# Seven block products for the second channel layer, its factors folded into weights and biases, in a sinkhorn-attention and ResMLP kernel

## The chip, the cores and the metric

The kernel runs on one core of one Trainium2 chip. The metric is the device time of one execution in microseconds (us). All runs were interleaved with runs of the kernel before, so each ratio compares runs of the same rounds. A run is called fast or slow by its time against the fastest of the same kernel; the slow ones here (three of e5_wtok, three of e18_wtok_nopool) showed a lower mean granted TensorE clock than the fast one beside them.

In the text PE is the matrix engine and PEld its weight load, DVE the vector engine, ACT the scalar engine, POOL the general engine. Work has to pass between them all the time: in this kernel PE's results go to accumulator banks (names in `_ps`, and `ch_a` to `ch_c` in the changed kernel), and ACT or DVE empties (evacuates) each bank before PE uses it again.

## The reference, cut to what matters

```python
# attention: x[b] (768 x 512), from 8 heads; 4 batches
a1  = alpha1 * x + beta1
tok = einsum('ts,bsd->btd', w_tok, a1)         # 768 x 768 token mixing
u   = x + lam * tok
a2  = alpha2 * u + beta2
ch  = maximum(a2 @ w_ch1, 0) @ w_ch2           # 512 -> 2048 -> 512
out = u + lam * ch
```

`lam`, the `alpha`s and the `beta`s are vectors of 512 channels.

## The kernel before

It works on batch 0's attention, then, for b = 1 to 3, on the attention of batch b laid between the matrix work of batch b-1 (hidden layer `h_ps`, second layer `ch_ps`), and at the end on batch 3's layers alone. The token mixing and both layers touched by the change, cut:

```python
def moe_tok(b, kts, done=False):               # kts: row tiles of 128 tokens
    for n in range(len(kts) + 1):
        if n < len(kts):
            if not done: tok_part(b, kts[n])   # 6 matmuls of 512 columns on x
            tps = tok_of[(b, kts[n])]
            dve.tensor_tensor(tps, tps, a1lB[:], ALU.mult)         # alpha1*lam
        if n > 0:
            kt = kts[n - 1]
            dve.tensor_tensor(u32[kt][:], tok_of[(b, kt)], u32[kt][:], ALU.add)
            act.copy(u16_of[b][:, kt, :], u32[kt][:])
# u32 holds x + beta1*lam*(row sums of w_tok) beforehand, computed by POOL
def moe_h(b, hf, which=range(HT)):             # hf: half of the rows, 384
    ...
        for ci in range(CT):                   # 4 matmuls of 384 columns
            pe.matmul(hps[:], W1p[:, ci, m*128:(m+1)*128], a2T_of[b][hf][:, ci, :], ...)
        act.activation(hT_of[(b, hf)][m], hps[:], AF.Relu)
def moe_ch(b, hf, kks=range(3)):
    ...
        for m in range(HT):                    # 16 matmuls of 512 columns
            pe.matmul(cps[:], hT[m][:, kk*128:(kk+1)*128], W2p[:, m, lo:hi], ...)
        dve.tensor_tensor(cps[:], cps[:], lamB[:, lo:hi], ALU.mult)
        dve.tensor_tensor(ost[:, lo:hi], cps[:], u_of[b][kt][:, lo:hi], ALU.add)
        ...                                    # two output DMAs
# batch 0 / batch 1, in PE's order:
    for kk in range(2):
        moe_ch(0, 0, (kk,))                    # second layer of batch 0 laid between
        mix_k(1, gs=((0, 1), (2,))[kk])        # batch 1's keys
        for h4 in range(2 * kk, 2 * kk + 2):
            turn_q(1, h4, dve.tensor_copy)     # and queries
```

The softmax here doesn't subtract the row's maximum and nothing guards it: scores larger than these inputs give would overflow.

## Time and profile before

| view | before |
|---|---|
| time, median (range) | 269.02 us (268.74 to 269.11) |
| busy share of PE / DVE / ACT / POOL | 96 / 58 / 47 / 35% |
| first real product of the opening (`pj_ps`) | 11.34 us |
| first `h_ps` | 42.5 us |
| first `v_ps` of batch 2 | 105.7 us |
| end of the last matmul, span | 262.5 us, 266.8 us |

The page's first part (busy time of each engine, share of the span, instructions), kernel before:

```profile
span 266.8 us, 5147 instructions
PE 257.3 (96%) x2049; PEld 141.6 (53%) x2059; DVE 154.8 (58%) x333; ACT 125.8 (47%) x232; POOL 92.6 (35%) x100
```

The chain of waits that ended last, as shares of the span by engine. It is almost all PE:

```profile
PE 89%; ACT 4%; DVE 4%; issue 1%; DMA 1%; DVEq 0%; ACTq 0%
```

Two stretches, from the first `h_ps` to batch 2's first `v_ps`, and from there to the last matmul. The columns are the stretch, its length, then each engine's busy time in it (number of instructions), and last the granted clock, the DMA share and GB/s:

```profile
42.50:105.70 63.20, 62.94 (x490) 34.68 (x493) 44.31 (x88) 30.45 (x58) 27.91 (x28) 1.00 1.04 154
105.70:262.50 156.80, 156.06 (x1059) 82.90 (x1062) 77.28 (x150) 71.12 (x134) 36.67 (x33) 1.00 0.50 81
```

PE idles 0.26 us in the first stretch and 0.74 us in the second, and `--waits` lists no wait of PE over its threshold of 0.15 us in either; DVE and ACT have a third to a half of the time free. Groups of instructions that the change touches (busy us, mean ns of one | idle time before them, and what ended it):

```profile
L65 ACT ACTIVATE hTa<-h_ps 128x384 bf16<-128x384 f32 x96 | 45.9, 492 | 67.7 <-PE h_ps L65 66.6
L65 DVE TENSOR_TENSOR ch_ps<-ch_ps,lamB 128x512 f32<-128x512 f32 (+2 forms) x25 | 16.9, 676 | 62.8 <-PE ch_ps L65 60.1 <-issue 2.6
L65 DVE TENSOR_TENSOR tok_ps<-tok_ps,a1lB 128x512 f32<-128x512 f32 x24 | 16.6, 693 | 7.7 <-PE tok_ps L65 7.6
L65 POOL TENSOR_SCALAR u<-b1lB,rs 128x512 f32<-128x512 f32 x18 | 28.9, 1612 | 64.7 <-DVE ost L65 60.1 <-ACT et L65 3.9 <-DVE red L65 0.6
```

The timeline of the opening (start, length, engine, operation, and in brackets the idle time just before and what ended it): the normalised matrix P is done by DVE, and PE, which has been idle, starts.

```profile
11.08 0.21 DVE L65 TENSOR_TENSOR P<-P,csum 32x64 f16<-32x64 f32 x1
11.34 0.34 PE L65 MATMUL pj_ps<-ident,P 32*8 32x8 f16 x8 [1.25 <-DVE P L65]
```

### The profile page before, as it was taken

Reading aid. Unit: us, or ns where it says so; the run is one execution under the profiler, and the core shown is the slowest. Engines: PE = TensorE matmul, PEld = TensorE weight load, DVE = VectorE, ACT = ScalarE, POOL = GpSimd, SP = SyncE. Lnnn points to the kernel's source line nnn. Section 1 sums busy time; section 2 is a strip of 40 time slices with the busy share of each in tenths; the row PEclk is TensorE's granted clock in tenths of the full one; section 3 lists DMA queues with packets and bytes.
Section 4 is the critical chain, followed back from the end, with each engine's and each line's share of the span. In section 5 each row is a group of like instructions: output and inputs, shape, how many; then the busy total and the mean of one; then the engine's idle time right before and its main releaser. Section 6 shows DMA issues by size and latency. Waiting matters only on the chain.

```text
span 266.8 us, 5147 instructions
## 1 busy us (share of the span) xinstructions
PE 257.3 (96%) x2049; PEld 141.6 (53%) x2059; DVE 154.8 (58%) x333; ACT 125.8 (47%) x232; POOL 92.6 (35%) x100
## 2 busy tenths in 40 slices
PE   7799999999999999999999999999999999999993
PEld 3467745565565444554565444554565445545542
DVE  6878687639567966722585867704675962042033
ACT  3376767642585312980375404970474305505600
POOL 8524789103585615008918125002409000000000
PEclk9999999999999999999999999999999999999999
DMA  6999999989999544499996342492200422012012
GB/s 80 183 208 252 206 211 207 209 209 118 206 165 146 115 83 120 115 83 95 207 196 135 61 100 80 118 109 51 81 1 2 86 71 79 2 39 79 2 39 79
DMA packets 62423, 30.88 MB, mean 116 GB/s; under 512 B 48888, under 2 KB 58112, under 8 KB 62400
## 3 DMA queue, kind: packets, MB, share of 16 engines
q0 software_dynamic: 23024, 15.60, 39.1%
q1 hardware_dynamic: 39376, 14.96, 32.7%
q8 instruction: 16, 0.26, 0.4%
q14 instruction: 7, 0.06, 0.1%
HBM read 32.78 MB, written 8.65 MB: 155 GB/s over the span
## 4 chain that ended last, share of the span: by engine, by line
PE 89%; ACT 4%; DVE 4%; issue 1%; DMA 1%; DVEq 0%; ACTq 0%
PE ch_ps L65 31%; PE h_ps L65 30%; PE tok_ps L65 12%; PE x_ps L65 5%; PE sc_ps L65 4%; ACT kT L65 2%; PE v_ps L65 2%; PE k_ps L65 1%; PE q_ps L65 1%; ACT et L65 1%; DVE csum L65 1%; DVE P L65 1%; PE m_ps L65 1%; DVE rsum L65 1%; PE wtok_ps L65 1%
## 5 line engine op out<-in xcount | busy, mean ns | idle before, releaser
L65 PE MATMUL h_ps<-a2T,W1p 128*128 128x384 bf16 x512 | 93.4, 326 | 0.2
L65 ACT ACTIVATE hTa<-h_ps 128x384 bf16<-128x384 f32 x96 | 45.9, 492 | 67.7 <-PE h_ps L65 66.6
L65 PE MATMUL ch_ps<-W2p,hTa 128*128 128x512 bf16 (+2 forms) x290 | 65.9, 370 | 0.5
L65 PEld LDWEIGHTS <-W1p 128*128 128x128 bf16 x512 | 47.5, 98 | 30.3 <-issue 0.9
L65 DVE TENSOR_TENSOR ch_ps<-ch_ps,lamB 128x512 f32<-128x512 f32 (+2 forms) x25 | 16.9, 676 | 62.8 <-PE ch_ps L65 60.1
L65 POOL TENSOR_SCALAR u<-b1lB,rs 128x512 f32<-128x512 f32 x18 | 28.9, 1612 | 64.7 <-DVE ost L65 60.1
L65 PEld LDWEIGHTS <-hTa 128*128 128x128 bf16 x300 | 28.7, 98 | 32.4
L65 PE MATMUL tok_ps<-x,w_tokT 128*128 128x512 f16 x144 | 32.1, 379 | 0.0
L65 POOL TENSOR_TENSOR u<-x,u 128x512 f32<-128x512 f16 x22 | 25.4, 1190 | 18.2 <-DVE x L65 17.3
L65 ACT ACTIVATE et<-sc_ps 96x768 f16<-96x768 f32 x32 | 24.9, 807 | 11.7 <-PE sc_ps L65 11.7
L65 ACT CAST u<-u 128x512 f16<-128x512 f32 x24 | 14.8, 618 | 25.7 <-DVE u L65 25.7
L65 PE MATMUL ch_ps<-W2p,hTb 128*128 128x512 bf16 (+2 forms) x100 | 25.0, 371 | 0.0
L65 PEld LDWEIGHTS <-w_tokT 128*128 128x128 f16 x180 | 14.8, 97 | 16.1
L65 DVE TENSOR_TENSOR tok_ps<-tok_ps,a1lB 128x512 f32<-128x512 f32 x24 | 16.6, 693 | 7.7 <-PE tok_ps L65 7.6
L65 DVE CAST kT<-k_ps 64x512 f16<-64x512 f32 x24 | 16.5, 688 | 3.4 <-PE k_ps L65 3.0
L65 DVE TENSOR_TENSOR x<-x_ps,recip 96x512 f16<-96x512 f32 (+2 forms) x32 | 17.6, 554 | 0.9
L65 DVE TENSOR_TENSOR u<-tok_ps,u 128x512 f32<-128x512 f32 x24 | 16.4, 689 | 1.7
L65 ACT ACTIVATE hTb<-h_ps 128x384 bf16<-128x384 f32 x32 | 15.3, 497 | 3.8 <-PE h_ps L65 3.4
L65 DVE TENSOR_TENSOR ost<-ch_ps,u 128x512 f32<-128x512 f32 (+2 forms) x25 | 16.6, 665 | 0.6
L65 POOL DMA_DIRECT2D qn<-in_q_dram x18 | 15.4, 872 | 4.2 <-PE q_ps L65 3.4
L65 PEld LDWEIGHTS <-hTb 128*128 128x128 bf16 x100 | 9.6, 98 | 10.9
L65 PEld LDWEIGHTS <-et 96*128 96x128 f16 (+2 forms) x288 | 12.4, 99 | 4.6 <-issue 1.2
(95 smaller groups left out, 214.0 us busy)
## 6 DMA issues: line engine op xcount, KB each, us to landing
out_dram<-ost SPq DMA_DIRECT2D x23, 192.0 KB, 2.2
raw<-in_v_dram POOLq DMA_DIRECT2D x8, 384.0 KB, 8.2
raw<-in_k_dram POOLq DMA_DIRECT2D x8, 384.0 KB, 10.7
vscr<-vA SPq DMA_DIRECT2D x6, 384.0 KB, 4.4
Vs<-vscr SPq DMA_DIRECT2D x6, 384.0 KB, 7.5
W1p<-in_moe_w_ch_dram POOLq DMA_DIRECT2D x4, 512.0 KB, 10.5
W2p<-in_moe_w_ch_dram POOLq DMA_DIRECT2D x4, 512.0 KB, 18.6
qn<-in_q_dram POOLq DMA_DIRECT2D x12, 128.0 KB, 5.8
```

What stands on the lines that cost most here:

```text
L65: ins = getattr(self.eng, name)(*args, **kwargs)
```

## The change

The intent is less work on PE, which is the bound. Take two row tiles of the hidden activations (2 x 2 blocks A11 to A22) and the 2 x 2 blocks B11 to B22 of W2: Strassen's scheme in Winograd's form needs seven block products in place of eight, at the price of four sums S1 to S4 per row pair and four combinations T1 to T4 of W2 once. For this lam is multiplied into W2 (scaled by 1024 to keep fp16 accurate), alpha2 into W1, and W1 times beta2 becomes a bias of the ReLU; `a1 = alpha1*lam*x + beta1*lam` is formed once per batch in fp16 (`xa`), so that one operation per tile finishes u. POOL has almost no tensor work left. Batch 0's attention is taken head pair by head pair. w_tok is no longer sorted by DVE but turned with 128-column loads and then 32-column loads over the tail. The core of the diff:

```diff
-                pe.transpose(pst[:, tt*128:(tt+1)*128], wtp[ks // 2][:, tt, ks % 2, :], ident16[:])
+            for rows, at in ((slice(0, 128), 96 * ks), (slice(96, 128), TAIL + 32 * ks)):
+                for tt in range(NT):
+                    pe.transpose(pst[rows, tt*128:(tt+1)*128],
+                                 wt16[:, tt, at:at + rows.stop - rows.start], ident16[:])
...
-    spin(psb([128, 512], FT, "spin_ps")[:], 7)     # fillers
+    spin(psb([128, 512], FT, "spin_ps")[:], 12)
...
+    def affine(b, lo, hi, eng, kts=slice(0, NT)):
+        eng.tensor_tensor(xa, x, a1l16..., ALU.mult)
+        eng.tensor_tensor(xa, xa, b1l16..., ALU.add)
...
+            for mm in range(2):                    # h_ps now 256 columns per m
+                act.activation(hT[:, m, :], hps[:, mm, :], AF.Relu, bias=hbias[:, m:m + 1])
...
+    def moe_sums(b, th):                           # 4 x 1024 elements on DVE
+        dve.tensor_tensor(S1, A21, A22, ALU.add)
+        dve.tensor_tensor(S2, S1, A11, ALU.subtract)
+        dve.tensor_tensor(A21, A11, A21, ALU.subtract)
+        dve.tensor_tensor(S4, A12, S2, ALU.subtract)
...
+        product(pa, A11, B11, True, False); take(u11, pa)   # 8 matmuls of 256 columns
+        product(pb, A12, B21, True, True);  take(u11, pb)   # take: u += ps/1024 on DVE
+        product(pa, S2, T2, False, False);  take(u12, pa)
+        product(pc, S1, T1, True, False);   take(u22, pc)
+        product(pa, S3, T3, False, False);  take(u22, pa)
+        product(pc, S4, B22, False, True);  take(u12, pc)
+        product(pa, A22, T4, False, True);  take(u21, pa)
...
-    for kk in range(2):
-        moe_ch(0, 0, (kk,))
-        mix_k(1, gs=((0, 1), (2,))[kk])
-        ... turn_q(1, h4, dve.tensor_copy)
+    for n in range(3):
+        mix_k(1, gs=(n,), share=(2, 0, 2))
+        turn_q(1, n, act.copy)
+        moe_h(0, 1, range(2 + n, 3 + n))
+    ...
+    for n in range(4): scale_w2(n)                 # W2 is ready only after this
+    combine_w2()
```

## The prediction

> **What bounds it now.** The page's busy table has PE at 96% of the span, DVE 58%, ACT 47%. The chain of waits is 89% PE: ch_ps 31%, h_ps 30%, tok_ps 12%. In that chain 64 h_ps matmuls of 384 columns take 10.40 us (162.5 ns each) and 36 tok_ps of 512 columns take 7.77 us (216 ns): 2.4 columns per ns plus about 2.5 ns per matmul. That agrees with the Trainium skill, "TensorE: Matmul & The Clock Gate" (section on 56 against 53.3 ns). Sixteen x_ps matmuls of 65 columns take 0.51 us, loads included, so loads hide behind 256 columns, which should cost about 109 ns. PE idles 1.3 us before pj_ps at 11.34 us, about 1 us in batch 0, about 2 us per batch 1 to 3 (at ACT kT), and 4 us of tail.
>
> **PE, removed and added.**
> - Second layer: 8 block products become 7; about 82.9 us of ch_ps becomes 672 x 109 = 73.4 us: -9.5.
> - h_ps: 512 x 162.5 becomes 768 x 109: +0.7.
> - w_tok: 36 more transposes of 128 moving columns: +2.0.
> - hbias: 64 one-column matmuls at 27.5 ns (as rs_ps: 36 in 0.99 us) +1.8, rs_ps -1.0.
> - Fewer filler matmuls and one q turn moved into the opening: -1.0.
> Net -7.0 us.
>
> **What takes it back.**
> 1. Opening: two 1x512 fp32 products (0.75 us each, as u<-b1lB,rs,x) enter the normalisation chain on DVE. pj_ps moves from 11.3 to about 12.7 us: +1.4.
> 2. DVE. Added: 48 sums of 128x1024, 4 W2 scalings and 4 combinations of 2048, the affine of x. The Trainium skill, "VectorE: DVE Perf Modes" (perf-mode tier table), gives tensor_tensor on 16-bit SBUF operands two elements per cycle; this trace has no such operation, but its 768-element fp16 copy from PSUM (545 ns) runs at that rate. Estimates: 0.69 us per sum (33 us), 1.2 us per W2 operation (10 us), affine 15 us, W1 scaling 3 us. 84 evacuations of 256 columns at 0.43 us (36 us) replace 33 us. Removed: one tok_ps pass (-16 us), a2T scaling and sorting (-12 us). DVE goes from 155 to about 186 us.
> 3. From the start of the first h_ps to the end of batch 1's tok and last ch, DVE has about 57 us of work against 57 us on PE, in bursts: the W2 block (10 us) precedes the first x_ps evacuations, and tok waits for the affine. I expect 4 to 6 us of new PE idle. In batches 2 and 3, reuse of bank ch_a waits for a DVE evacuation within 0.87 us.
> ACT (about 140 us) and POOL (under 30 us) stay off the chain.
>
> **Sum.** 269.0 - 7.0 + 1.4 + about 5 (batch 0/1) + about 1 - 3 (idle of batches 2 and 3 partly removed) = about 266. Range 260.5 to 270.5. Chances: faster by over 2% 0.33, within 2% 0.60, slower 0.07.
>
> **What would show it.** ch_ps groups total about 73 us at 109 ns spacing; pj_ps near 12.7 us; first h_ps near 45.5 us (42.6 before); batches 2 and 3 take about 57 us (58.7); last batch's h and ch about 40 us (41.5); DVE near 186 us, sums near 0.69 us; waits of PE loads on DVE (u, x, xa) grow.
>
> **What would make it wrong.** Sums or W2 operations at one element per cycle: slower. DVE bursts hidden better than I think: about 260. Loads not hidden at 256 columns: 275 or more.

## The result, and the profile after

The changed kernel took 276.92 us (median of four fast runs, 276.13 to 277.49) against 269.05 us for the kernel before in the same rounds: ratio 1.029, 95% interval 1.026 to 1.032. A ratio here is the mean time of one kernel's fast runs over that of the other's of the same rounds, so it is not quite the ratio of the medians. The prediction had 266.0 us, 0.989 of before; the result is 6 us above the top of its range. The profiled executions have spans of 266.8 and 275.7 us, 8.9 us apart.

The page's first part, kernel after:

```profile
span 275.7 us, 6448 instructions
PE 260.1 (94%) x2693; PEld 201.5 (73%) x2693; DVE 177.7 (64%) x384; ACT 146.4 (53%) x303; POOL 37.3 (14%) x54
```

The chain of waits: PE has lost 19 points of the span, and DVE and ACT have gained 18, although they are busy for only 64 and 53% of it.

```profile
PE 70%; DVE 14%; ACT 12%; issue 2%; POOL 0%; ACTq 0%; POOLq 0%; DVEq 0%
```

The same two stretches:

```profile
47.20:114.50 67.30, 61.42 (x621) 47.34 (x621) 52.12 (x100) 38.44 (x80) 8.47 (x11) 1.00 0.88 120
114.50:271.60 157.10, 153.56 (x1471) 123.35 (x1468) 93.36 (x193) 84.96 (x184) 7.84 (x11) 1.00 0.59 82
```

PE idles 5.88 us in the first (0.26 before) and 3.54 us in the second (0.74). The groups that answer to those of before:

```profile
L66 ACT ACTIVATE hT<-h_ps,hbias 128x256 f16<-128x256 f32 x192 | 77.7, 489 | 25.1 <-PE h_ps L66 23.5
L66 DVE SCALAR_TENSOR_TENSOR u<-ch_a,u 128x256 f32<-128x256 f32 x48 | 20.1, 420 | 8.4 <-PE ch_a L66 8.3
L66 DVE TENSOR_TENSOR S<-S,hT 128x1024 f16<-128x1024 f16 x12 | 8.2, 681 | 0.1
L66 DVE TENSOR_TENSOR xa<-x,a1l 128x768 f16<-128x768 f16 (+1 forms) x9 | 7.3, 816 | 0.0
L66 DVE TENSOR_TENSOR W2p<-W2p,lam 128x2048 f16<-128x2048 f16 x4 | 4.6, 1221 | 0.0
```

The opening. P is ready 1.3 us later than before, as predicted; but twelve filler matmuls already stand in PE's queue in front of `pj_ps`, which starts 1.5 us after P is done.

```profile
11.39 2.76 PE L66 MATMUL spin_ps<-ident 128*128 128x512 f16 x12
12.40 0.21 DVE L66 TENSOR_TENSOR P<-P,csum 32x64 f16<-32x64 f32 x1
14.08 0.34 PE L66 MATMUL pj_ps<-ident,P 32*8 32x8 f16 x8
```

PE's waits in the whole run, the longest in total first, cut (us in all, times, longest):

```profile
PE ch_a L66 <- DVE u L66: 2.7, 6, 0.7
...
PE h_ps L66 <- ACT hT L66: 1.1, 1, 1.1
PE ch_a L66 <- DVE S L66: 1.1, 1, 1.1
```

And a piece of the chain just before batch 1's first `tok_ps` at 100.57 us (start, length, what), which shows the new kind of bound: one DVE operation after the other from three different jobs (evacuations u and x, sums S, affine xa), with PE only at the end.

```profile
95.25 0.56 DVE S L66
95.80 0.34 DVE x L66
96.14 0.33 DVE xs L66
96.47 0.60 DVE S L66
97.07 0.34 DVE u L66
...
98.15 0.69 DVE S L66
98.85 0.47 DVE xa L66
99.31 0.34 DVE u L66
...
99.70 1.03 PE ch_a L66 x8
```

Where the 8.9 us lie, by first starts in the timeline and the busy time in the stretches:

| stretch | before | after | difference | predicted |
|---|---|---|---|---|
| start to `pj_ps` | 11.3 | 14.1 | +2.7 | +1.4 |
| `pj_ps` to first `h_ps` | 31.1 | 33.1 | +2.0 | +1.8 |
| PE busy, first `h_ps` to last matmul | 219.0 | 215.0 | -4.0 | -8.8 |
| PE idle, the same | 1.0 | 9.4 | +8.4 | +3 |
| after the last matmul | 4.3 | 4.1 | -0.2 | 0 |

(The second row's prediction is the prediction's w_tok, hbias, rs_ps and filler terms together; the third its -9.5 and +0.7; the fourth its "about 5 + about 1 - 3".)

More than half of the shortfall in the third row lies between the products. Eight matmuls of 256 columns take 1.04 us in the record but follow each other at 0.87 us (97.58 to 98.45 us in the timeline): the record has a tail of about 0.16 us, and so much of every stop counts as busy. Adding up from one matmul's start to the next, less the idle time in the record, the second layer took about 83.3 us before and 76.6 after, where 672 x 109 ns would be 73.2: the per-matmul price was right. Of the other 3.3 us, 1.8 are the hidden first part of eleven stops that show idle time as well, 0.35 are five stops shorter than the tail, and about 1 us lies where PE goes from a product to other work.

### The profile page after: what moved, and what is told of

Read it like the earlier page. It is cut to its first block, busy times and chain, and to the rows that moved or that the text cites. A ratio compares the mean times of both kernels' runs of the same rounds, so it can differ in the third digit from the quotient of the medians.

```text
span 275.7 us, 6448 instructions
## 1 busy us (share of the span) xinstructions
PE 260.1 (94%) x2693; PEld 201.5 (73%) x2693; DVE 177.7 (64%) x384; ACT 146.4 (53%) x303; POOL 37.3 (14%) x54
## 4 chain that ended last, share of the span: by engine, by line
PE 70%; DVE 14%; ACT 12%; issue 2%; POOL 0%; ACTq 0%; POOLq 0%; DVEq 0%
PE h_ps L66 21%; PE ch_a L66 11%; PE tok_ps L66 11%; PE ch_c L66 6%; ACT hT L66 5%; PE sc_ps L66 4%; PE spin_ps L66 4%; DVE x L66 3%; PE x_ps L66 3%; DVE u L66 3%; ACT et L66 3%; DVE xa L66 3%; ACT kT L66 2%; DVE S L66 2%; PE wtok_ps L66 2%
## 5 line engine op out<-in xcount | busy, mean ns | idle before, releaser
L66 PE MATMUL h_ps<-uT,W1p 128*128 128x256 f16 x768 | 92.9, 273 | 2.5 <-ACT hT L66 1.1
L66 ACT ACTIVATE hT<-h_ps,hbias 128x256 f16<-128x256 f32 x192 | 77.7, 489 | 25.1 <-PE h_ps L66 23.5
L66 PEld LDWEIGHTS <-W1p 128*128 128x128 f16 x832 | 74.2, 98 | 14.1 <-issue 2.9
L66 PEld LDWEIGHTS <-hT 128*128 128x128 f16 x384 | 37.2, 98 | 6.9 <-issue 1.8
L66 PEld LDWEIGHTS <-S 128*128 128x128 f16 x288 | 27.8, 98 | 8.0 <-issue 3.1
L66 PE MATMUL tok_ps<-xa,w_tokT 128*128 128x512 f16 (+1 forms) x180 | 32.0, 336 | 0.0
L66 PE MATMUL ch_a<-W2T,hT 128*128 128x256 f16 x192 | 25.4, 272 | 1.3 <-DVE u L66 1.3
L66 PE MATMUL ch_c<-W2p,S 128*128 128x256 f16 x192 | 26.2, 273 | 0.4 <-DVE S L66 0.2
L66 DVE SCALAR_TENSOR_TENSOR u<-ch_a,u 128x256 f32<-128x256 f32 x48 | 20.1, 420 | 8.4 <-PE ch_a L66 8.3
L66 DVE SCALAR_TENSOR_TENSOR u<-tok_ps,x 128x512 f32<-128x512 f32 x24 | 16.2, 688 | 11.4 <-PE tok_ps L66 11.2
## 6 DMA issues: line engine op xcount, KB each, us to landing
raw<-in_k_dram POOLq DMA_DIRECT2D x8, 384.0 KB, 13.9
```

The lines of the kernel that those rows point to most:

```text
L66: ins = getattr(self.eng, name)(*args, **kwargs)
```

## The experiments

The first theory, from the trace: in the stage of batches 0 and 1 there are two limits one after the other. From 57 to 79 us it is ACT (busy 20.5 of 22 us), because W2 is not yet scaled, and PE can fill its gaps only with `h_ps`, of which each needs two ReLUs; from 84 to 101 us it is DVE (busy 16.1 of 17 us), with sums, affine and evacuations. In batches 2 and 3 the waits for DVE take what the seven products gain. Rivals: the block of W2 operations (as I had predicted), ACT alone, DVE alone, PE itself (loads not hidden, w_tok).

The last 17 us up to batch 1's first `tok_ps`, in the kernel before and in the changed kernel (PE is the first busy time, DVE the third):

```profile
68.10:85.10 17.00, 16.99 (x198) 10.32 (x197) 11.82 (x30) 12.78 (x23) 9.53 (x11) 1.00 1.39 170
84.00:101.00 17.00, 14.85 (x154) 11.87 (x153) 16.08 (x40) 1.61 (x2) 0.00 (x0) 1.00 0.57 91
```

All runs, against the kernel before of the same rounds (268.8 to 269.05 us):

| run | median (range) us | ratio to before | result |
|---|---|---|---|
| changed kernel | 276.92 (276.13 to 277.49) | 1.029 | correct |
| e1_spin5 | 276.62 (275.82 to 278.38) | 1.030 | correct |
| e2_qk_dve | 277.47 (276.32 to 279.78) | 1.033 | correct |
| e3_no_w2 | 277.22 (276.95 to 277.46) | 1.031 | wrong |
| e4_plain | 279.88 (279.33 to 280.25) | 1.040 | correct |
| e5_wtok | 279.19 (the one fast run), 3 slow | - | correct |
| e6_pool_aff | 293.35 (291.69 to 294.40) | 1.087 | correct |
| e7_hybrid | 285.10 (284.33 to 285.32) | 1.057 | correct |
| e8_qk_paff | 292.95 (292.73 to 293.20) | 1.087 | correct |
| e9_hybrid_dve | 276.16 (275.77 to 276.33) | 1.027 | correct |
| e10_relu_wide | 276.35 (274.56 to 277.18) | 1.027 | reference met, though a bias was left out |
| e11_dve_light | 270.91 (270.68 to 271.48) | 1.008 | wrong |
| e12_both | 270.37 (268.94 to 270.87) | 1.004 | wrong |
| e13_no_sums | 273.44 (272.88 to 275.29) | 1.019 | wrong |
| e14_no_affine | 273.34 (272.81 to 273.61) | 1.017 | wrong |
| e15_hybrid_spin5 | 275.64 (274.88 to 277.98) | 1.026 | correct |
| e16_relu_share | 275.97 (274.38 to 276.03) | 1.025 | correct |
| e17_pe_only | 269.12 (268.90 to 270.49) | 1.001 | wrong |
| e18_wtok_nopool | 278.26 (the one fast run), 3 slow | - | correct |

The opening is not the same in every execution (see e1_spin5), so the traces are also compared from the first `h_ps` to the last matmul: 220.0 us before, 224.4 in the changed kernel, 227.4 in e4_plain, 223.4 in e9_hybrid_dve, 224.0 in e10_relu_wide, 218.7 in e11_dve_light, 217.2 in e12_both, 220.8 in e13_no_sums, 220.7 in e14_no_affine, 217.5 in e17_pe_only.

### e1_spin5: the fillers

```diff
-    spin(psb([128, 512], FT, "spin_ps")[:], 12)
+    spin(psb([128, 512], FT, "spin_ps")[:], 5)
```

> The changed kernel with 5 filler matmuls instead of 12 in front of pj_ps. In its trace the matrix P16 is ready at 12.6 us, but pj_ps starts at 14.1 us, behind fillers still in the PE queue. Theory A (the fillers are the delay): pj_ps at about 12.7 us and the whole kernel 1.2 to 1.6 us faster than the changed one (about 275.4). Rival (the delay is swallowed by a later wait, DMA or DVE): pj_ps earlier, but less than 0.5 us gained at the end.

`pj_ps` started at 12.70 us, at once when P was done:

```profile
12.44 0.21 DVE L66 TENSOR_TENSOR P<-P,csum 32x64 f16<-32x64 f32 x1
12.70 0.34 PE L66 MATMUL pj_ps<-ident,P 32*8 32x8 f16 x8 [0.22 <-DVE P L66]
```

Every later milestone of the trace is 1.4 us earlier, up to the last matmul (270.2 against 271.6 us). So in these two executions the opening's excess over my +1.4 is the seven fillers. It varies: in the traces of the fifteen kernels with twelve fillers `pj_ps` starts 0.05 to 1.65 us after P is done, in the four with five fillers 0.05 to 0.06 us. The timed median fell by only 0.3 us; the granted clock of two of its four runs was 0.988 and 0.991 (278.38 and 277.10 us), and the two at 0.997 and 0.998 took 275.82 and 276.14.

### e2_qk_dve: batch 1's q and k copies back on DVE

```diff
-        mix_k(1, gs=(n,), share=(2, 0, 2))
-        turn_q(1, n, act.copy)
+        mix_k(1, gs=(n,), share=(4, 0, 4))
+        turn_q(1, n, dve.tensor_copy)
```

> The changed kernel with the copies of batch 1's q and k out of PSUM put where the kernel before has them (qT on DVE, kT with shares 4, 0, 4). It takes 5.5 us from ACT and gives DVE 5.0 us, just before the W2 block. Theory A (from 47 to 75 us ACT is the limit: it is busy 24.5 of 27.7 us there): 2 to 4 us faster than the changed kernel, idle PE in 47 to 75 us falls from about 6 to 2 or 3 us. Rival B (DVE with its 9.6 us W2 block is the limit): no gain, or up to 2 us slower, because the block starts later.

PE's idle time from 60 to 80 us fell from 2.5 to 0.8 us and batch 1's first `x_ps` came 1.4 us earlier, but its first `tok_ps` only 0.6 us. DVE was busy 4.91 of the 5 us before 100 us, PE only 2.08, and the clock then fell to 0.50 for the next 5 us. (This execution was the slowest of its four, 279.78 us.) What ACT had cost there was won and DVE took it back before `tok_ps`. It agrees with two limits in series, and it is no gain.

### e3_no_w2: no W2 operations

```diff
-    for n in range(4):
-        scale_w2(n)
-    combine_w2()
+    # and T2, T3, T4 = B22, B11, B21
```

> Wrong result on purpose: the W2 block (four scalings and four combinations on DVE, 9.6 us) is left out, and products take the unscaled blocks of W2; PE work is unchanged. Theory A (ACT is the limit before 75 us): the first x_ps still comes at about 79 us, and only the second half (75 to 101 us) gains, because DVE is not behind any more; 0 to 2 us in all. Rival B (the DVE block is the limit): 4 to 7 us faster, about 271.

The result is wrong (relative error 0.020). All milestones stood within 0.1 us of the changed kernel's (`x_ps` 79.0, `tok_ps` 100.5 against 100.6), and the time was the same. The 10 us block of W2 operations on DVE that my prediction put ahead of the first `x_ps` costs nothing.

### e4_plain: the second layer as eight products

```diff
-        product(pa, A11, B11, True, False)  ...  # seven products, four sums
+        for m in range(HT):                      # 16 matmuls of 512 columns per row tile
+            pe.matmul(cps[:], hT[:, m, r*128:(r+1)*128], W2p[:, m, :], ...)
```

> The changed kernel with a plain second layer: 16 matmuls of 512 columns per 128 tokens, no sums, no combinations; everything else (folded scales, affine, ReLU bias, batch 0 by head pair, 256-token tiles) stays. PE gets about 9.5 us more work, DVE about 55 us less. If the seven products pay what they save on PE: 7 to 9.5 us slower than the changed kernel (about 285). Theory A (the PE time saved is mostly lost to waits on DVE and ACT, and the loss is in the rest of the change): within 3 us of the changed kernel, 275 to 280; last batch's h and ch 41.5 us, batches 2 and 3 about 59 us.

At 279.88 us the plain layer is 3.0 us slower than the seven products. So of the 9.5 us of PE work that they save 3 us arrive: batches 2 and 3 are 59.5 and 59.6 us long between their first `tok_ps` (`tok_ps` to `tok_ps`; 58.1 and 58.9 with the seven products), the last stage, to the last matmul, 56.5 against 54.0. Up to batch 1's first `tok_ps`, though, the plain layer is 1.6 us faster (51.7 us after the first `h_ps`, in place of 53.4): up to there the seven products do not pay. The rest of the change, without Strassen, costs about 11 us against the kernel before. There too W2 is scaled late.

### e5_wtok and e18_wtok_nopool: w_tok sorted on DVE, as before

```diff
+            sort_wtok(0)                 # two DVE copies per pair of blocks, 3 pairs
...
-            for rows, at in (...):  ... 12 transposes per block
+            for tt in range(NT): pe.transpose(..., wtp[ks // 2][:, tt, ks % 2, :], ident16[:])
```

In e18_wtok_nopool, in addition, `aff0(0, pool)` became `aff0(0, dve)`.

> The changed kernel with w_tok sorted by DVE and turned by 36 loads of 128 columns, as the kernel before does, instead of 72 loads with 32 columns over the tail. PE saves 36 matmuls of 128 moving columns (0.88 us per group of 12 against 0.46 us for 6 in the kernel before: 2.5 us), DVE gets 2.6 us. If batch 0's attention is limited by PE: bias_ps starts about 2 us earlier (35 us), first h_ps about 45.2 us, 1.5 to 2.3 us faster in all. Rival (DVE or ACT sets that stage): less than 0.5 us gained.

> Correct kernel: w_tok sorted by columns on DVE and turned with 36 loads as in the kernel before, and the first part of batch 0's affine on DVE, so that POOL runs no tensor operation beside DVE's copies. If the 36 extra transposes of the change are what costs in batch 0 (2 us of PE), the first h_ps comes 1 to 2 us earlier than in the changed kernel with pj_ps at the same place, total 275 to 276. If DVE has no room for 6 us more there, pv waits for it and the first h_ps comes no earlier or later by up to 2 us, total 277 to 279. The stretch at half clock of the earlier run must not come back if POOL's operation was its cause.

In e5_wtok PE stopped for 2.15 us at 25.6 us, waiting for DVE's sorted columns. The first of those DVE copies took 1.38 us (0.45 to 0.81 us in the kernel before) while POOL ran its affine. Then the clock was halved. Windows of 3 us of this (slow) execution; PE is the first busy time, the granted clock the third number from the end:

```profile
25.00:28.00 3.00, 0.85 (x17) 0.67 (x18) 2.97 (x6) 0.37 (x1) 2.92 (x4) 1.00 1.24 206
28.00:31.00 3.00, 3.00 (x36) 2.28 (x34) 1.11 (x3) 1.58 (x2) 1.85 (x3) 0.50 1.24 207
31.00:34.00 3.00, 3.00 (x37) 2.19 (x35) 1.88 (x5) 0.99 (x3) 0.57 (x1) 0.50 1.17 222
```

e18_wtok_nopool took POOL out of it. From `pj_ps` to the bias products it was 22.3 us against 22.8, so about 0.5 us of the 36 transposes came back, but DVE was busy 3.86 of the 4 us from 24 us on, PE idled 1.3 us there and 0.9 us from 32 to 37, the clock was 0.57 from 37 to 41, and the first `h_ps` came at 47.7 us, 0.5 later than in the changed kernel. Three of its four runs were slow. My expectation of a return of 1 to 2 us missed; DVE has no room for the sorting in this order. Turning w_tok by 128- and 32-column loads costs PE 2.4 us by its starts (5.28 us against 2.91), near the +2.0 predicted; it is part of the loss, but not of the miss.

### e6_pool_aff and e8_qk_paff: the affine on POOL

```diff
-            affine(b, lo, hi, dve)
+            affine(b, lo, hi, dve if lo == 384 else pool)
```

e8_qk_paff adds the edit of e2_qk_dve.

> The changed kernel with three quarters of the affine of batches 1 to 3 (columns 0 to 383) on POOL, which is idle there; DVE keeps columns 384 to 511. Takes about 2 us per batch from DVE. Theory C (from 84 us to the start of batch 1's tok DVE is the limit: it is busy without a gap from 84 to 101 us): tok of batch 1 starts 1 to 2 us earlier, batches 2 and 3 0.3 to 0.7 us shorter each, 1.5 to 3 us faster in all. Rival (ACT alone delays batch 1, or the last POOL operation now ends later than DVE did): 0 to 0.5 us.

> e2 and e6 together: q and k copies of batch 1 off ACT, and three quarters of the affine off DVE. e2 alone brought batch 1's first x_ps 1.4 us forward but its tok only 0.6 us. If ACT (to 79 us) and DVE (84 to 101 us) are two limits in series: tok of batch 1 starts 2 to 3.5 us earlier than in the changed kernel, about 97.5 us, more than e2 and e6 give one by one, and 2 to 4 us faster in all, unless the TensorE clock falls as it did in e2's profile (0.5 from 100 to 105 us). Rival (something else starts tok): at most the gain of e6.

Both were 16 us slower than the changed kernel, at a granted clock of 0.965 to 0.973, so a part of it is clock. The timeline of e6_pool_aff shows where it begins: three DVE copies that take 0.69 us together in the changed kernel took 4.04, until POOL's operation was over.

```profile
85.83 3.08 POOL L66 TENSOR_TENSOR xa<-x,a1l 128x1536 f16<-128x1536 f16 x1 [9.62 <-DVE x L66]
85.94 0.69 DVE L66 TENSOR_TENSOR x<-x_ps,recip 96x512 f16<-96x512 f32 x1
88.34 4.04 DVE L66 COPY x<-xs 32x256 f16<-32x256 f16 x3
88.99 3.08 POOL L66 TENSOR_TENSOR xa<-xa,b1l 128x1536 f16<-128x1536 f16 x1
```

The Trainium skill, "SBUF — State Buffer" (section "SBUF: two separate sides"), says that DVE and POOL share a port pair as an exclusive lock, held for a whole instruction, and that it touches DVE operations in a two-port mode, or with two SBUF inputs if POOL's operation reads SBUF. This trace agrees. An evacuation from an accumulator bank beside a POOL operation (second line) keeps its time of 0.69 us. So the question that these two runs were for stayed open: POOL was no free helper for DVE.

### e7_hybrid and e9_hybrid_dve: batch 0's second layer plain

```diff
-    mix_k(1, gs=(n,), share=(2, 0, 2)); turn_q(1, n, act.copy); moe_h(0, 1, ...)
+    mix_k(1, gs=(0,)); turn_q(1, 0, act.copy); plain_ch(0, 0)
+    mix_k(1, gs=(1,)); turn_q(1, 1, dve.tensor_copy); moe_h(0, 1, range(1))
+    mix_k(1, gs=(2,)); turn_q(1, 2, act.copy); plain_ch(0, 1); turn_q(1, 3, dve.tensor_copy)
+    # W2 is scaled between the v evacuations of batch 1, on DVE
+    # (e7_hybrid: two of the four groups on POOL); combine_w2() after batch 0
```

> Batch 0's second layer plain and in the place where the kernel before has it: W2 scaled early (two groups on DVE between the v_ps copies, two on POOL), then 32 second-layer matmuls of 512 columns between the k and q work of batch 1, where the changed kernel has h_ps matmuls; batches 1 to 3 keep the seven products, with the combinations made after batch 0. PE gets 2.4 us more work. Theory D (in 57 to 79 us the changed kernel has only first-layer matmuls to fill PE with, each of which needs ACT, while ACT also turns k and q): from first h_ps to batch 1's tok, counted with the same second-layer work, 4 to 6 us less idle PE; 2 to 4 us faster in all (273 to 275). Rival (the loss is in DVE after 84 us or elsewhere): no gain or slower.

> Batch 0's second layer is plain again (six 512-column row blocks, W2 scaled on DVE between the v evacuations, nothing on POOL), so PE again has work without any ACT step to lay between k_ps, q_ps and the scores of batch 1; the seven products start with batch 1. Theory (in that stage ACT's ReLUs, q, k and exponentials are the limit because W2 is not ready): the first h_ps to first tok_ps of batch 1 falls from 53.4 us to about 50, first h_ps to batch 2's first v_ps from 67.3 to 64 to 65, total 274 to 275. Rival (DVE's added work alone is the limit): the four W2 scalings come earlier but DVE has the same sum of work, so first h_ps to batch 2's v_ps stays at 67 or grows by the 2.4 us that six plain blocks cost more than three times seven products; total 277 to 279.

e7_hybrid met the same lock: POOL's two W2 operations ran 8.10 us, and a DVE operation of 128 x 128 elements that takes 0.29 us in the kernel before took 3.5 us.

```profile
45.71 8.10 POOL L66 TENSOR_TENSOR W2p<-W2p,lam 128x2048 f16<-128x2048 f16 x2 [6.62 <-DMA W2p<-in_moe_w_ch_dram]
46.37 3.52 DVE L66 TENSOR_TENSOR bigP<-mskb,red 128x128 f16<-128x128 f16 x1
```

e9_hybrid_dve is the test without POOL. In the stage of batches 0 and 1, and from there to the last matmul:

```profile
46.50:113.30 66.80, 65.94 (x578) 42.84 (x578) 44.55 (x80) 37.58 (x80) 7.53 (x11) 1.00 0.94 130
113.30:269.90 156.60, 150.62 (x1440) 120.28 (x1440) 93.06 (x192) 82.52 (x179) 7.55 (x11) 1.00 0.49 79
```

PE's idle time there fell from 5.88 to 0.86 us, the first `tok_ps` came 48.4 us after the first `h_ps` in place of 53.4, better than the 50 expected. So a filler that needs little from ACT was missing. (The edit also takes 7.6 us of work off DVE in that stage. It is not what filled PE before the first `x_ps`: in 22 us there PE is busy 21.8 us in this run, 18.7 in e11_dve_light, where DVE has less to do, and 18.75 in the changed kernel.) But the stage as a whole shrank by 0.5 us, not by 2 to 3, because PE now had 2.4 us more to do for the plain layer, and did some 3 us of batch 1's `h_ps` early (28 more matmuls in the stretch); the next stage was 1.5 us shorter for it and the one after 0.9 us longer. The time fell by 0.8 us. Of the 5.0 us of idle time won, 1.6 were exchanged for work and 2.4 came back as idle time later (5.98 us in place of 3.54), with one stop of 2.70 us in which batch 2's first `tok_ps` waits for DVE's xa.

### e10_relu_wide, e11_dve_light, e12_both: relieve ACT, DVE, both

```diff
# e10: one ReLU for two column blocks (one bias for both)
+            act.activation(hT[:, 2*n:2*n+2, :], hps[:], AF.Relu, bias=hbias[:, 2*n:2*n+1])
# e11: no S sums (S1, S2, S4 = A21, A22, A12; S3 = A21), no affine in batches 1 to 3 (xa = x)
# e12: both
```

> Wrong result on purpose (one hidden-layer bias for two column blocks): each pair of ReLUs of 256 columns becomes one of 512, which takes about 10 to 20 us off ACT in the whole run and nothing off DVE or PE. Theory (two limits in series, ACT from 57 to 79 us and DVE from 84 to 101 us): batch 1's first x_ps comes 1.5 to 2.5 us earlier than 79.0, but its first tok_ps only 0 to 1.5 us earlier than 100.6; batches 2 and 3 lose under 0.7 us each; total 274 to 276. Rival (ACT alone is the limit): tok_ps and the end follow x_ps in full and batches 2 and 3 gain 1.5 us each, total 270 to 272. Rival (DVE alone): nothing moves, 276 to 277.

> Wrong result on purpose: the S sums and the affine of batches 1 to 3 are left out, which takes about 40 to 45 us off DVE and nothing off ACT or PE. Theory (series): batch 1's first x_ps stays within 0.7 us of 79.0, its first tok_ps comes 2 to 4 us earlier, the waits of ch_a for DVE fall away so batches 2 and 3 gain 1 to 1.5 us each; total 269 to 272. Rival (ACT alone): tok_ps moves under 1 us, total 275 to 277. Rival (DVE alone): everything is won, x_ps earlier too, total 266 to 268.

> Wrong result on purpose: both lightenings at once. Theory (series): the gains at x_ps and at tok_ps add up, first tok_ps of batch 1 at 95 to 97 us, batches 2 and 3 about 57 us each as I had predicted for the changed kernel itself, total 265 to 268; that is more than the sum of the two single gains. If PE work alone (its loads, its bank reuse) were the cause, even this kernel stays at 273 or more.

e10_relu_wide took 12.5 us off ACT's busy time, but its ReLUs overlap less: one of 512 columns takes 691 ns where two of 256 follow each other at about 365 ns each, so it is a weak relief. It still shows in the stretch from 57 to 79 us, first the changed kernel, then e10_relu_wide:

```profile
57.00:79.00 22.00, 18.75 (x223) 15.58 (x222) 17.20 (x21) 20.48 (x44) 8.47 (x11) 1.00 1.40 130
```

```profile
57.00:79.00 22.00, 20.32 (x249) 17.05 (x249) 16.52 (x20) 19.52 (x31) 7.46 (x11) 1.00 1.45 140
```

PE did 1.6 us more there, as ACT's limit demands, and the median fell by 0.6 us. The first `tok_ps` came where it had come (100.5 us), but that does not show that DVE took the gain back: in this execution the clock was 0.50 from 95.9 to 99.3 us, and 16 second-layer matmuls took about 0.21 us each in place of 0.11, some 1.6 us in all. Its two runs at a clock of 0.99 took 277.0 and 277.2, the two near 1.0 took 275.7 and 274.6, where the changed kernel's three at 1.0 took 276.1 to 277.2. So ACT's part may be about 1.5 us.

e11_dve_light took 36.5 us off DVE, and 6.0 us off the time; the change had lost 7.9. Its idle time by stretches:

```profile
46.10:112.60 66.50, 62.47 (x634) 48.63 (x634) 42.47 (x85) 38.85 (x81) 8.39 (x11) 1.00 0.92 129
112.60:264.90 152.30, 150.96 (x1458) 122.39 (x1456) 66.33 (x149) 84.88 (x184) 7.61 (x11) 1.00 0.53 83
```

The second stretch, from batch 2 to the end, is 4.8 us shorter than in the changed kernel, and PE idles 1.34 us in it in place of 3.54; the waits of `ch_a` for DVE's u are gone from it. In the first stretch the idle time is 4.03 us in place of 5.88. e12_both is only 0.5 us faster than e11_dve_light by the medians, and 1.5 us from the first `h_ps` to the last matmul (its trace has `pj_ps` 0.9 us later). I had expected 265 to 268 us, more than the two reliefs give one by one; about 1.5 us (by the runs near full clock) and 5.7 us one by one and 7.1 together look like two causes that add up, so the theory of two equal limits in series falls. DVE's additions are the main cause, in batches 2 and 3 as well, and ACT's part is small.

### e13_no_sums, e14_no_affine: which DVE work

```diff
# e13: only the S sums left out
+        S1, S2, S4 = A21, A22, A12
# e14: only the affine of batches 1 to 3 left out
-            affine(b, lo, hi, dve)
```

> Wrong result on purpose: only the S sums are left out (33 us of DVE), the affine stays. If what costs is the sums, which have to be done between the last ReLU and the products and so lie across the evacuations that free the product's banks: batches 2 and 3 gain 1.5 to 2 us each, total 271.5 to 273. If it is the affine, which stands between the last x_ps evacuation and tok_ps: total 275 to 277.

> Wrong result on purpose: only the affine of batches 1 to 3 is left out (about 11 us of DVE), the sums stay. If it is the affine that costs: first tok_ps of batch 1 comes 2 to 3 us earlier, total 271 to 273. If the sums: tok_ps moves by under 1.5 us, total 274.5 to 276.5. The two single gains should add to about the 6 us of both together; if they add to much less, either one alone gives DVE enough room.

The sums are worth 3.5 us and the affine 3.6 us; 7.1 together, against 6.0 for both at once. So neither alone is the cause, and per microsecond of DVE time the affine (DVE's busy time fell by 9.1 us without it) costs three times what the sums do (27.3 us). My reading of why: the affine stands between the last evacuation of x and `tok_ps`, where nothing else is ready (the stop of 2.70 us in e9_hybrid_dve is such a wait), while sums can run during other products. That this makes the threefold price is not shown.

### e15_hybrid_spin5, e16_relu_share: do the valid gains add, and does ACT limit batches 2 and 3

```diff
# e15: e9_hybrid_dve with 5 fillers
# e16: e15, and every fourth ReLU of the first two row pairs of batches 1 and 2 on DVE
+                    dve.tensor_scalar(hT[:, m, :], hps[:, mm, :], hbias[:, m:m+1], 0.0,
+                                      op0=ALU.add, op1=ALU.max)
```

> Correct kernel: plain second layer in batch 0 and 5 fillers in place of 12 before pj_ps. If the gains add (0.8 us and 1.4 us against the changed kernel): 274.5 to 275.5. If the 1.4 us is lost later, because the next stage waits for something else: 276 or more.

> The kernel of the run before, and in addition every fourth ReLU of the first two row pairs of batches 1 and 2 on DVE (16 of 64 per batch and so some 6 us less on ACT, 7 us more on DVE). If ACT limits the first third of batches 2 and 3, they get 0.5 to 1 us shorter each, total 273 to 274.5. If DVE's sum of work over the batch is what limits, they get 0.5 to 1.5 us longer each, total 276 to 278.

e15_hybrid_spin5 took 275.64 us, 1.3 less than the changed kernel and not the full sum of 0.8 and 1.4: its runs at a clock of 0.997 and 0.998 took 274.9, those at 0.991 and 0.985 took 276.4 and 278.0. e16_relu_share made the stage from batch 2's `v_ps` to batch 3's 0.9 us shorter in the trace and the next one 0.1 longer; the timed runs do not tell it from e15_hybrid_spin5. That is inconclusive for ACT in batches 2 and 3, and at most a small gain. Neither comes near the kernel before.

### e17_pe_only: all reliefs at once

e15_hybrid_spin5 with neither S sums nor affine; wrong.

> Wrong result on purpose: plain second layer for batch 0, 5 fillers before pj_ps, and neither S sums nor affine in batches 1 to 3. If the three causes are the whole miss and independent, total 275.6 - 6.0 = about 269.5; if the filler work and the DVE room replace each other (both end the same idle time in the stage of batches 0 and 1), 270.5 or more; if they help each other, 268 or less. PE work alone would put it near 266 (my prediction without its waits, plus 2.4 for the plain batch).

It took 269.12 us, the time of the kernel before and within 0.4 us of what independent causes add up to. So the three reliefs together remove 7.8 of the 7.9 us by which the change was slower, and they are nearly independent. It is no valid kernel, and against the prediction it is not the whole miss.

```profile
45.70:112.50 66.80, 65.93 (x578) 42.79 (x578) 41.09 (x76) 37.58 (x80) 7.53 (x11) 1.00 0.95 133
112.50:263.20 150.70, 149.35 (x1440) 120.56 (x1440) 66.38 (x148) 82.67 (x179) 7.55 (x11) 1.00 0.51 82
```

PE's idle time is 2.2 us here in the two stretches. Even so the run is 3 us above the 266 that I had for PE work alone. In the two stretches PE was busy 215.3 us: 3.7 less than before, where my terms (-8.8, and +2.4 for the plain batch) give 6.4 less. Longer turns of batch 0's u and batch 1's q are about 1.1 us of that difference by the timeline's starts; the rest, about 1.6 us, is short stops and `h_ps`, not settled further.

## Why the prediction was wrong

Right:
- The price of a 256-column matmul (109 ns), of a sum (0.69 us predicted, 0.68 to 0.69 measured), of a W2 operation (1.2 predicted, 1.22 measured). The Trainium skill, "VectorE: DVE Perf Modes" ("The perf-mode tier table"), gives 1224 ns for a 2048-element 16-bit `tensor_tensor`; the trace's 1221 ns agrees.
- P ready 1.3 us later (+1.4 predicted). Batch 0 2.0 us longer (+1.8), in part by luck: the fillers there went from six to eight (+0.65 us by their starts) where a saving stood, and 0.9 us less idle time made up for it.
- The new idle time in the stage of batches 0 and 1: 4 to 6 us predicted, 5.6 measured (5.88 less 0.26).

Wrong, in the order of size:
1. The step that failed is the last term of the sum, "about 1 - 3 (idle of batches 2 and 3 partly removed)", and with it the last sentence on batches 2 and 3 in point 3. It takes off 3 us of idle time that was not there: the prediction has "about 2 us per batch 1 to 3 (at ACT kT)", but the profile before shows 0.74 us from batch 2 to the end and 1.00 us in both stretches. (ACT kT has 2% of the chain of waits, about 5 us; that I took this share for idle time of PE is likely, not shown.) And the new waits were priced at about 1 us. So from batch 2 to the end I let PE gain 2 us of idle time; it lost 2.8 (0.74 to 3.54 us). With both stretches together I had +3, measured +8.4. The runs show waits for DVE in its place: without sums and affine that stretch is 4.8 us shorter and idles 1.34 us. I had put the added DVE work into a total (186 us; 177.7 measured) and compared totals, 58% to 64% busy; but sums, affine and seven evacuations per row pair come one after the other in a burst at the end of each attention: DVE was busy 16.1 of the last 17 us before batch 1's `tok_ps`, and 15.2 and 13.9 of 17 before those of batches 2 and 3 (11.4 to 11.8 in the kernel before).
2. "PE, removed": -8.8 us after the first `h_ps`, measured -4.0. The seven products' matmuls cost what I said, but about 3 us lie between the products, most of it the part of stops that the tail of the records hides, and turns of u and q in batches 0 and 1 cost about 1 us more. Of the 9.5 us of Strassen, e4_plain shows 3 arriving.
3. "Fewer filler matmuls": I counted 1.0 us off, with a q turn. There are more of them, not fewer: twelve in place of seven in front of `pj_ps`, eight in place of six in batch 0. The twelve stand in PE's queue and hold `pj_ps` up to 1.65 us past P, 1.5 us in the changed kernel's trace. e1_spin5 shows that.
4. In point 3 the amount was right and its cause was not: the W2 block costs nothing (e3_no_w2), and "ACT stays off the chain" was wrong: ACT is 12% of it. What was missing was filler work that needs no ACT (e9_hybrid_dve: idle 5.88 to 0.86 us). The kernel before had it in the second layer, laid between q and k; the change has W2 ready too late for that.

The Trainium skill, "ScalarE: Activation LUTs" ("What ACT_TABLE_LOAD costs"), gives about (N + 335)/1.2 ns for an activation with a pointer bias, 492 ns for 256 columns; the trace has 489 ns. The 384-column ReLUs of before took 492 to 497 ns, without a bias. So cutting 384 columns to 256 and adding a bias bought nothing per instruction and made 192 of 128: ACT's ReLUs went from 61.2 to 77.7 us. I could have costed that beforehand.

What stays open: the 1.6 us of e17_pe_only named there, and whether another order of the DVE work would keep the seven products' gain. Since no valid version came below 275.6 us, none beats the kernel before.

## What to carry to other kernels

When a change takes work from the busiest engine and gives it to helpers, do not compare totals: list, for the stretch where the helper's bursts fall, every operation that the busiest engine's next bank or operand waits for. Smaller matmuls also shorten the time in which the helpers' answers can hide (0.87 us per product here, against two DVE operations), so a saving in matrix columns can turn into waits. And look at what filled a stage's gaps before: work that is moved later, or made to need another engine, leaves those gaps open.

## What the Trainium skill lacked or had wrong

- "TensorE: Matmul & The Clock Gate" ("HAM oscillation — how this bites in real kernels") gives as rule that PE should have no idle gaps over about 3.4 us. Here the length of a gap alone did not decide. After one stop of 2.15 us in e5_wtok (a slow execution) the clock was 0.50 from 28.0 to 38.2 us while PE was busy all the time; it was 0.50 for 3.4 us after stops of 0.48 and 1.14 us in e10_relu_wide, and two losses of 1.3 and 0.9 us in e18_wtok_nopool were followed by 0.57. But after a stop of 2.70 us in e9_hybrid_dve, and one of 3.60 us in e6_pool_aff, it stayed at 1.00. The page says that the start of a kernel varies from run to run; it does not say that whole runs differ by the clock lost later: e15_hybrid_spin5 took 274.9 us at a mean clock of 0.998 and 278.0 at 0.985.
- "SBUF — State Buffer" has the lock between DVE and POOL, and the runs agree. Its one size for a DVE victim is a factor of 6.8 without the operations; here three copies of 0.69 us took 4.04 us, and an operation of 0.29 us took 3.5 us, each until the POOL operation (3 to 4 us long) ended.
- "Perfetto Trace Analysis" says that the ends of matmuls in a trace are estimated and that their busy time is a poor measure, but not how much a busy share can hide: eight matmuls of 1.04 us in the record follow each other at 0.87 us, so 0.16 us of each stop counts as busy, some 2 us between the products of this kernel.
